# Attention and two mixers on one core: five loads issued ahead of the sixth pair's q and k, and the third pair's score bank opened without twelve products of zeros

## The chip, the core and the metric

The kernel runs on one core of a Trainium2 chip. The metric is the device time of one execution in microseconds; the median of three runs counts. TensorE (PE) multiplies into PSUM banks, VectorE (DVE), ScalarE (ACT) and GpSimd (POOL) work on what it leaves, and SyncE (SP) issues nearly all transfers, in order, to 16 DMA engines.

## The reference

Attention over 4 batches, 8 heads, 576 tokens and 64 numbers a head, once on means of four tokens (repeated to full length) and once on a band of tokens less than 4 apart, the two added; then a mixer over tokens and channels, then a second one with cosines and sines:

```python
out_d = sm_attn(q_d, k_d, v_d)                   # means of 4 tokens
out_up = np.repeat(out_d, factor, axis=2)
mask = np.abs(pos[:, None] - pos[None, :]) < factor
scores = np.where(mask, scale * q @ k.T, -1e9)
out_local = softmax(scores) @ v
x = out_up + out_local                           # (4, 576, 512)
h = relu(xt @ w_tok1) @ w_tok2;  u = x + h.T     # moe
x = u + relu(u @ w_ch1) @ w_ch2
theta = x @ w_theta
y = w_tok_r @ (x * cos(theta)) + w_tok_i @ (x * sin(theta))
out = (x + y) + relu((x + y) @ w_ch)             # moe2
```

The weights come as float64, which the kernel reads as pairs of 32-bit words and turns into float32 itself.

## The kernel before

The attention goes by pairs of heads: 16 pairs, four to a batch. Two pairs make a quad. The work of each pair and quad is cut into steps, written as generators, and the string ORDER (L33) says in which order the steps are taken; the program's instructions stand on each engine in just that order (L1131). A name in ORDER takes the next piece of its step; `L0*2` takes two. The letters that matter here, with the pairs counted from 0, so that pair 5 is the sixth:

- `P5` is load_pair(5) (L375): one transfer of q and k, 128 rows of 1164 float32, into one of four buffers `qk`. The loads stand in the order P0 P1 P4 P2 P3 P5, so P5 is the sixth and takes the buffer of pair 1. It must wait until pair 1's q and k have been read, by pool_pair (DVE) and by the score products (PE).
- `W0` is load_values(0) (L382): four transfers of the values of pair 0, two of 32 rows and two of 6, 1170 float32 each, into one of two buffers `vw`.
- `G0`, `G1` and `G6` are weights of the token mixer (converted, L166): their first piece issues a transfer of float64 (128 rows of 512 words for G0 and G1, of 288 for G6), the later ones turn it into float32 on ACT, DVE and POOL.
- `V1` is pool_values(1) (L391): its first piece loads 128 rows of 1300 float32, the later ones add them up on POOL.
- `K5` is pool_pair(5) (L413): two additions on DVE (L421 and L422) that make sums of four tokens of q and k.
- `F0`, `F1` are quad_front (L425): pooled scores `sd`, their maximum `mxd` (L452), exponentials `pd` (ACT), transpositions `pdt` (L477, L482), the pooled output `od` (L493 to L500), its division `ods` (L504 to L507), and its write and reload (L510 to L519).
- `L1`, `L2`, `L3` are pair_local (L522): local scores `s` of pair 1, 2, 3 in a PSUM room, their maximum and exponentials in `pbuf`, transpositions `pt` (L558), local output `o` (L568).

pair_local opens the room with warm(), which multiplies zeros WARM[n] times into columns that nobody reads, then puts the mask into the room (L530), then adds 40 score products (L533). Each of those is float32 and stands as two products with two weight loads in the trace:

```python
        s = wide(f"s_{at}")
        warm(s[:, 0, 192:512], WARM[n])
        for j in range(2):
            pe.matmul(s[:, j, 0 : NB * W], id16, msk, start=True, stop=False)
        yield
```

The rooms `s`, `sd`, `pdt`, `pt` and `o` come from one pool of two, so each waits until the one before last has been read.

Transfers on SP carry one of eight semaphores, DMAHW0 to DMAHW7, in turn. A transfer waits until the one that had its semaphore before it, eight places ahead, has landed.

Of the kernel before, what the change touches and what calls it, by code (L numbers as in the profile page):

```python
# [30 lines left out]
FIRST = 1  # L31
ROWS = ((8, 9), (0, 2), (4, 6), (2, 3))
ORDER = """  # L33
G3 P0 G2 I*2 P1 G3 P4 G3 V0 P2 G3 K0 G3 G2 I G2 I L0*2 P3 K1 F0 W1 L0 F0 L1 L0 G3 F0 V0 L1*2 P5 V0 L2 W0 G2 K2 V0 G2
F0 G1 L1 V1 F0 L2 K3 G0 G6 K4 L0 F0 L0 L2 L1 G2 F1 L2 K5 L1 L0 F0 F1 G1*2 F1 V1 F0*2 W3 L0 F1 G5 G0 L1 G0 F1 G6 F2 L1
G0 P6 W2 G5 G6 L3 V1 F2 V1 L3 G6 F2 F1 L3 G1 G4 F1 L2 P7 L5 L2 L5 F1 G1 L3 A0 V2 X0 A1 T0 L3 G1 L5 G0 L3 T0 G0 L2 G2
F1 G4 F2 G5 T0 K6 T0 V2 X2 L2 G6 W5 F2 K7 V2 L4*2 E0.0*2 T0 L4 V3 V2 A2 L3 E0.1 L5 G4 L4 W4 L5 G6 L5 G4 L3 X2 F3 G5 P8
P9 A3 G4 F2 G5 E0.1 T1 G4 G5 T0 F2 V3 L4 F3 F2 T0 L4 V3 X2 F3 L6 V3 L6 X7 T0 P11 L6 X2 X0 F3 K8 U0.0 L6 T0 X2 X0 U0.0
# [49 lines left out]
LOWER, WIDE = 2, 2  # L88
MIX = 384
NMIX = 6  # L90
WARM = [24] + [12] * 3 + [0] * 12
DEEP = [4, 4]

B, H, S, D = 4, 8, 576, 64
# [20 lines left out]
def kernel(  # L115
# [177 lines left out]
    def wide(name):  # L293
        return big.tile([128, 2, 512], F32, tag="big", name=name)
# [17 lines left out]
    def warm(out, k):  # L312

        for _ in range(k):
            pe.matmul(out, zero[:, 0:128], zero[:, 0 : out.shape[-1]], start=True, stop=True)
# [206 lines left out]
    def pair_local(n):  # L522
# [4 lines left out]
# [3 lines that stand above are left out]
# [928 lines left out]
```

## Time and profile before

| | us |
|---|---|
| median of three runs | 680.91 (680.24 to 683.12) |
| the profiled execution | 686.51 |
| its span, first to last instruction | 684.7 |
| TensorE busy | 657.2 (96%) |
| VectorE busy | 521.0 (76%) |
| ScalarE busy | 321.1 (47%) |

The profiled execution is one of its own; its time is a little over the median. A row of the timeline gives the start, the time that it took, the engine, the source line, the operation, what it writes and reads, how many instructions were merged, and in brackets the idle time of the engine just before and what ended it. "issue" stands there where the engine waited for nothing that the profile shows. SPq is SP's queue of transfers; its rows give the issue, not the landing. PEclk is the granted clock of TensorE as a share of 2.4 GHz; 0.50 is 1.2 GHz. The attention fills the first part of the span, about 180 us, with the token mixer and the weights mixed in; the rest belongs to the channel mixer and the second mixer.

### The profile page before, as it was taken

How to read it: one execution, taken by the hardware profiler on the slowest of the kernel's cores; microseconds unless marked ns; L12 is line 12 of the kernel's file. 1: busy time of each engine (PE TensorE's matmuls, PEld its weight loads, DVE VectorE, ACT ScalarE, POOL GpSimd, SP SyncE). 2: the span in 40 equal slices, each digit the busy share in tenths (PEclk: the TensorE clock that was granted, in tenths of full speed). 3: DMA queues.
4: the chain of work that ended last, by engine and by line, in shares of the span. 5: the costliest groups of instructions: out<-in, count | busy, mean ns of one | idle time of the engine just before them, and what ended most of it. 6: DMA issues, size and time to landing. Idle time of an engine off the chain costs nothing.

```text
span 684.7 us, 17393 instructions
## 1 busy us (share of the span) xinstructions
PE 657.2 (96%) x7320; PEld 627.6 (92%) x7320; DVE 521.0 (76%) x952; ACT 321.1 (47%) x632; POOL 98.0 (14%) x92
## 2 busy tenths in 40 slices
PE   7678898999999999999999999999999999999997
PEld 4457788989999999999999999999999998998997
DVE  5789997878462679898987886668798848857837
ACT  4466657466252556434624423253657326526311
POOL 3034220604200242300200210012000000000000
PEclk9899999999999999999999999999999999999999
DMA  8688886777441866625353853599620240140202
GB/s 280 198 273 238 255 250 237 209 243 242 137 146 53 285 232 211 226 76 145 128 150 102 279 133 95 178 335 284 169 62 1 75 149 1 61 140 1 70 1 69
DMA packets 93021, 109.93 MB, mean 161 GB/s; under 512 B 46880, under 2 KB 69536, under 8 KB 92944
## 3 DMA queue, kind: packets, MB, share of 16 engines
q1 hardware_dynamic: 92080, 106.08, 49.8%
q0 software_dynamic: 864, 2.75, 1.0%
q8 instruction: 57, 0.93, 0.6%
q14 instruction: 20, 0.16, 0.1%
HBM read 79.13 MB, written 29.69 MB: 159 GB/s over the span
## 4 chain that ended last, share of the span: by engine, by line
PE 83%; DMA 6%; DVE 5%; ACT 3%; SPq 1%; issue 1%; DVEq 0%; ACTq 0%
PE y L158 6%; PE y L157 6%; PE y L159 6%; PE c L158 4%; PE c L157 4%; PE c L159 4%; PE c L699 4%; PE c L702 4%; PE c L700 4%; PE c_p L903 3%; PE c_p L905 3%; PE c_p L902 3%; PE th L158 2%; PE th L157 2%; PE th L159 2%; DMA qk<-qkT 2%
## 5 line engine op out<-in xcount | busy, mean ns | idle before, releaser
L158 PE MATMUL y<-wrl,zh 128*128 128x288 f32 x256 | 74.9, 296 | 0.0
L157 PE MATMUL y<-wrh,zh 128*128 128x288 f32 x256 | 74.8, 296 | 0.0
L159 PE MATMUL y<-wrh,zl 128*128 128x288 f32 x256 | 71.9, 295 | 0.0
L219 POOL TENSOR_TENSOR ww<-ww,raw 128x512 int32<-128x512 int32 (+2 forms) x30 | 41.1, 1373 | 161.8 <-DMA raw<-w_ch 55.6
L157 PEld LDWEIGHTS y<-wrh,zh 128*128 128x128 f32 x256 | 48.0, 188 | 0.0
L158 PEld LDWEIGHTS y<-wrl,zh 128*128 128x128 f32 x256 | 48.0, 188 | 0.0
L159 PEld LDWEIGHTS y<-wrh,zl 128*128 128x128 f32 x256 | 46.9, 188 | 0.0
L219 POOL TENSOR_TENSOR raw<-raw 128x512 int32<-128x512 int32 (+2 forms) x16 | 20.0, 1248 | 139.0 <-DVE raw L215 57.5
L1231 DVE TENSOR_TENSOR cx<-y,cx 128x288 f32<-128x288 f32 x32 | 14.6, 457 | 32.3 <-PE y L159 31.7
L151 ACT CAST cuh<-cx 128x288 fp32r<-128x288 f32 (+1 forms) x16 | 8.8, 553 | 59.5 <-DVE cx L1231 59.5
L199 ACT ACTIVATE ww<-raw 128x512 f32<-128x512 f32 (+2 forms) x30 | 19.4, 647 | 27.1 <-DVE c1l L223 9.5
L921 DVE SCALAR_TENSOR_TENSOR g<-c,g 128x384 fp32r<-128x384 f32 x40 | 21.1, 551 | 13.9 <-ACT g L918 13.8
L157 PE MATMUL th<-thh,cxh 128*128 128x512 f32 (+1 forms) x92 | 31.6, 343 | 0.0
L158 PE MATMUL th<-thl,cxh 128*128 128x512 f32 (+1 forms) x92 | 31.6, 343 | 0.0
L918 ACT ACTIVATE g<-c 128x384 fp32r<-128x384 f32 x40 | 19.1, 490 | 25.5 <-PE c L159 25.5
L159 PE MATMUL th<-thh,cxl 128*128 128x512 f32 (+1 forms) x92 | 31.1, 343 | 0.0
L201 ACT ACTIVATE raw<-raw 128x512 int32<-128x512 uint32 (+3 forms) x46 | 29.4, 639 | 0.0
L929 DVE TENSOR_TENSOR ut<-c,ut 128x384 f32<-128x384 f32 x32 | 17.1, 551 | 9.9 <-PE c L702 9.9
L533 PE MATMUL s<-qk 64*32 64x38 f32 x1280 | 16.1, 205 | 6.1 <-issue 6.1
L533 PEld LDWEIGHTS s<-qk 64*32 64x32 f32 x1280 | 13.6, 105 | 8.8 <-issue 8.4
L157 PE MATMUL t<-w2h,h 128*128 128x256 f32 (+1 forms) x64 | 21.5, 337 | 0.0
L157 PE MATMUL c<-uh,c1h 128*128 128x384 f32 x64 | 21.4, 334 | 0.0
(390 smaller groups left out, 2270.5 us busy)
## 6 DMA issues: line engine op xcount, KB each, us to landing
raw<-w_ch SPq DMA_DIRECT2D x27, 512.0 KB
qk<-qkT SPq DMA_DIRECT2D x16, 582.0 KB
xT<-ut SPq DMA_DIRECT2D x12, 768.0 KB
vd<-vtok SPq DMA_DIRECT2D x8, 650.0 KB
vw<-vloc SPq DMA_DIRECT2D x32, 146.2 KB
uT<-us SPq DMA_DIRECT2D x16, 288.0 KB
ut<-uT SPq DMA_DIRECT2D x6, 768.0 KB
ut<-xT SPq DMA_DIRECT2D x6, 768.0 KB
```

The lines of the kernel that those rows point to most:

```text
L157: pe.matmul(out, lh, rh, start=start, stop=False, skip_group_check=again)
L158: pe.matmul(out, lh, rl, start=False, stop=False, skip_group_check=again)
L159: pe.matmul(out, ll, rh, start=False, stop=stop, skip_group_check=again)
L201: act.activation(f, words[:, :, 0], AF.Copy, scale=2.0**-29)
L219: pool.tensor_tensor(out=w.bitcast(I32), in0=w.bitcast(I32), in1=f, op=ALU.add)
L533: pe.matmul(s[r : r + 32, j, i // 2 * W : i // 2 * W + W], q[64 * j : 64 * j + 64, 32 * g : 32 * g + 32], k[64 * j : 64 * j + 64, 32 * g : ...
L699: pe.matmul(ps[:, 0:MIX], h[:, cb % 2, d], h1, start=cb == cbs[0], stop=False)
L700: pe.matmul(ps[:, 0:MIX], l[:, cb % 2, d], h1, start=False, stop=False)
L702: pe.matmul(ps[:, 0:MIX], weight[cb // 2][2][:, cb % 2, d], h2, start=False, stop=cb == cbs[-1])
L902: pe.matmul(ps[:, 0:MIX], h[:, cb % 2, d], h1, start=cb == cbs[0], stop=False)
L903: pe.matmul(ps[:, 0:MIX], l[:, cb % 2, d], h1, start=False, stop=False)
L921: dve.scalar_tensor_tensor(out=h2, in0=ps, scalar=0.0, in1=h1.bitcast(F32), op0=ALU.max, op1=ALU.subtract)
```

## The change

Two edits. In ORDER, P5 stands later: behind W0, which followed it, and behind the first pieces of G1, G0, G6 and V1, which are pulled forward to stand with it. That makes five steps that issue loads ahead of P5, eight transfers in all. WARM gives pair 2 no products of zeros:

```diff
-G3 P0 G2 I*2 P1 G3 P4 G3 V0 P2 G3 K0 G3 G2 I G2 I L0*2 P3 K1 F0 W1 L0 F0 L1 L0 G3 F0 V0 L1*2 P5 V0 L2 W0 G2 K2 V0 G2
-F0 G1 L1 V1 F0 L2 K3 G0 G6 K4 L0 F0 L0 L2 L1 G2 F1 L2 K5 L1 L0 F0 F1 G1*2 F1 V1 F0*2 W3 L0 F1 G5 G0 L1 G0 F1 G6 F2 L1
+G3 P0 G2 I*2 P1 G3 P4 G3 V0 P2 G3 K0 G3 G2 I G2 I L0*2 P3 K1 F0 W1 L0 F0 L1 L0 G3 F0 V0 L1*2 V0 L2 W0 G1 G0 G6 V1 P5
+G2 K2 V0 G2 F0 L1 F0 L2 K3 K4 L0 F0 L0 L2 L1 G2 F1 L2 K5 L1 L0 F0 F1 G1*2 F1 V1 F0*2 W3 L0 F1 G5 G0 L1 G0 F1 G6 F2 L1
-WARM = [24] + [12] * 3 + [0] * 12
+WARM = [24, 12, 0, 12] + [0] * 12
```

On SP, behind the values of pair 1, before (the names in brackets are the semaphores waited for; qk_1 is the sixth pair's q and k, vw_0 the values of pair 0, raw the weights, vd_1 the pooled values, od_0 the first pooled output):

```order
L378 DMA qk_1_347<-qkT 128x1164 [waits DMAHW6_49,DVE_49,PE_49]
L387 DMA vw_0_366<-vloc 32x1170 [waits DMAHW7_49]
L387 DMA vw_0_366<-vloc 32x1170 [waits DMAHW0_49]
L387 DMA vw_0_366<-vloc 6x1170 [waits DMAHW1_49]
L387 DMA vw_0_366<-vloc 6x1170 [waits DMAHW2_49]
L187 DMA raw_393<-w_tok 128x2x256 [waits DMAHW3_49]
L396 DMA vd_1_396<-vtok 128x1300 [waits DMAHW4_49,Pool_49]
L187 DMA raw_444<-w_tok 128x2x256 [waits DMAHW5_49]
L187 DMA raw_446<-w_tok 128x288 [waits DMAHW6_49]
L510 DMA od_0_57<-ods_0_572 4x32x256 [waits DMAHW7_49,DVE_49]
```

And now, at the same place:

```order
L387 DMA vw_0_352<-vloc 32x1170 [waits DMAHW6_49]
L387 DMA vw_0_352<-vloc 32x1170 [waits DMAHW7_49]
L387 DMA vw_0_352<-vloc 6x1170 [waits DMAHW0_49]
L387 DMA vw_0_352<-vloc 6x1170 [waits DMAHW1_49]
L187 DMA raw_357<-w_tok 128x2x256 [waits DMAHW2_49]
L187 DMA raw_359<-w_tok 128x2x256 [waits DMAHW3_49]
L187 DMA raw_361<-w_tok 128x288 [waits DMAHW4_49]
L396 DMA vd_1_363<-vtok 128x1300 [waits DMAHW5_49,Pool_49]
L378 DMA qk_1_365<-qkT 128x1164 [waits DMAHW6_49,DVE_49,PE_49]
L510 DMA od_0_57<-ods_0_560 4x32x256 [waits DMAHW7_49,DVE_49]
```

The sixth pair's load moved from the first place to the last but one, each of the others one or more places ahead; with its place each transfer changed its semaphore, and so the landing that it waits for.

On TensorE, between the scores of pair 1 and those of pair 2, before:

```order
L533 MATMUL s_1_278<-qk_1_148 32x38 x39
L315 LDWEIGHTS zero [waits DVE_49]
L315 MATMUL s_2_351<-zero 128x320 [waits Activation_49]
...
L530 MATMUL s_2_351<-fixed,id_121 128x190
L477 MATMUL pdt_0_379<-fixed,pd_0_296 128x128 [waits DVE_49,PE_49]
L477 MATMUL pdt_0_379<-fixed,pd_0_296 128x128 x4
L482 MATMUL pdt_0_379<-fixed,pd_0_296 32x128 x8
```

And now:

```order
L533 MATMUL s_1_278<-qk_1_148 32x38 x39
L530 LDWEIGHTS id_121 [waits DVE_49]
L530 MATMUL s_2_349<-fixed,id_121 128x190 [waits Activation_49]
L530 LDWEIGHTS id_121
L530 MATMUL s_2_349<-fixed,id_121 128x190
L477 MATMUL pdt_0_375<-fixed,pd_0_296 128x128 [waits DVE_49,PE_49]
L477 MATMUL pdt_0_375<-fixed,pd_0_296 128x128 x4
L482 MATMUL pdt_0_375<-fixed,pd_0_296 32x128 x8
```

The waits of the first product of zeros went over to the mask's; the transposition's own wait for DVE and PE stayed. On DVE, ACT and POOL the attention's steps stand in the same order as before.

## Rows read from the trace of the kernel before

**Rows 1.** Busy time by stretches: us, each engine's busy (count), PEclk, DMA share, GB/s
```profile
20.00:25.00 5.00, 2.34 (x17) 1.51 (x21) 1.39 (x4) 0.71 (x3) 0.00 (x0) 0.61 1.02 335
25.00:30.00 5.00, 4.81 (x177) 4.06 (x169) 4.11 (x9) 2.38 (x6) 1.60 (x1) 0.71 0.19 64
...
110.00:120.00 10.00, 10.00 (x158) 9.37 (x158) 7.81 (x13) 8.25 (x18) 0.36 (x1) 1.00 0.68 248
```

**Rows 2.** Chain of waits in order of time, 19 to 40 us: start, us, what
```profile
19.04 3.63 issue
...
29.02 0.76 DVE mxd L452
...
35.58 4.70 DMA raw<-w_tok
```

**Rows 3.** Timeline of TensorE's products, 14.9 to 33 us
```profile
14.90 0.31 PE L533 MATMUL s<-qk 64*32 64x38 f32 x17 [0.94 <-issue]
15.14 1.80 PE L315 MATMUL s<-zero 128*128 128x320 bf16 x12
...
16.95 0.71 PE L477 MATMUL pdt<-fixed,pd 128*128 128x128 f32 x5
...
18.16 0.88 PE L533 MATMUL s<-qk 64*32 64x38 f32 x76
22.66 0.34 PE L533 MATMUL s<-qk 64*32 64x38 f32 x4 [3.63 <-issue]
...
32.46 0.76 PE L477 MATMUL pdt<-fixed,pd 128*128 128x128 f32 x5 [2.65 <-ACT pd L473]
```

**Rows 4.** The page: TensorE's counts, instruction queue; that queue from 19.5 to 21.5
```profile
PE 657.2 (96%) x7320; PEld 627.6 (92%) x7320; DVE 521.0 (76%) x952; ACT 321.1 (47%) x632; POOL 98.0 (14%) x92
...
q8 instruction: 57, 0.93, 0.6%
...
q8 instruction: 1, 0.02, 4.1%
```

**Rows 5.** TensorE by microseconds: us, busy (count), PEclk, DMA share, GB/s
```profile
15.00:16.00 1.00, 1.00 (x24) 1.00 0.17 51
...
22.00:23.00 1.00, 0.34 (x5) 0.50 1.06 417
```

**Rows 6.** Timeline of SP, 9 to 45 us: start and time of the issues
```profile
9.87 1.61 SPq L387 DMA_DIRECT2D vw<-vloc  x4
15.31 0.36 SPq L378 DMA_DIRECT2D qk<-qkT  x1
...
18.30 2.26 SPq L187 DMA_DIRECT2D raw<-w_tok  x2
28.27 0.62 SPq L510 DMA_DIRECT2D od<-ods  x1
...
35.58 0.77 SPq L187 DMA_DIRECT2D raw<-w_tok  x1
```

**Rows 7.** Timeline of VectorE, GpSimd and ScalarE, 15 to 41 us
```profile
15.90 0.55 DVE L546 TENSOR_TENSOR pbuf<-s,mx 128x380 f32<-128x380 f32 x1
...
19.73 0.46 DVE L422 TENSOR_TENSOR qkd<-qa 128x288 f32<-128x288 f32 x1
...
25.15 0.75 DVE L421 TENSOR_TENSOR qa<-qk 128x576 f32<-128x576 f32 x1
25.49 1.60 POOL L398 TENSOR_TENSOR vd<-vd 128x650 f32<-128x650 f32 x1 [10.04 <-DMA vd<-vtok]
25.94 1.48 DVE L422 TENSOR_TENSOR qkd<-qa 128x288 f32<-128x288 f32 x1
...
27.75 0.49 DVE L507 TENSOR_TENSOR ods<-od,rd 128x320 f32<-128x320 f32 x1
...
40.30 0.46 ACT L199 ACTIVATE ww<-raw 128x288 f32<-128x288 f32 x1 [4.72 <-DMA raw<-w_tok]
```

**Rows 8.** Waits of SP's queue, 9 to 30 us: us, times, longest
```profile
SPq L187 <- DMA qk<-qkT: 1.5, 1, 1.5
```

## Prediction

> **What bounds the kernel now.** I read the busy time by stretches first. From 110 us on TensorE has no idle time [rows 1], so what happens there is its own work, which the change does not touch. Before that it has, and in the first 45 us a step that comes earlier can bring the rest forward. So I read the chain of waits there [rows 2]. It goes through a stall of 3.63 that the profile calls issue, the maximum of the second pooled scores on VectorE at 29.02, and a load of token weights issued at 35.58 that is waited for 4.70 long. The twelve products of zeros for the third pair lie just ahead of the stall [rows 3].
>
> The stall at 19.04 is not a wait for data: it cuts the 80 products of the third pair's scores into 76 and 4 [rows 3]. From the end of an earlier such gap (14.90) to 19.04 there are 17 + 12 + 2 + 5 + 16 + 76 = 128 products, each with its weight load: 256 instructions. In the whole run the instruction queue q8 moves 57 packets for TensorE's 14640 products and weight loads, 257 each; one of them falls between 19.5 and 21.5 us [rows 4]. So TensorE takes its instructions in blocks of 256, and here it had run out of one. It took 4.1% of 16 engines over 2 us, 1.3 us of one engine, so it was there between 20.8 and 21.5 and TensorE went on 1.2 to 1.9 later.
>
> The DMA engines ran dry just before: at 15 us their share is 0.17 [rows 5], since SP sat from 11.48 to 15.31 at the sixth pair's load [rows 6]. That load needs the buffer of the second pair, whose last reader is the score products that end at 15.21.
>
> **The change part by part.**
>
> *Twelve products of zeros removed.* They take 1.80 on TensorE [rows 3], all of it on the chain. But the next instruction but two is the transposition of the first pooled exponentials, which waits for VectorE too: its bank is the second pair's, whose last reader is the subtraction of 15.90, done at 16.45 [rows 7]. It started at 16.95 [rows 3] and can now start at 16.5. So 0.45 is gained here, not 1.80.
>
> *The block's edge.* 24 instructions fewer put the edge behind the 4 products that were cut off (8 instructions), the five transpositions of the first pair (10) and three products of the pooled output (6). The third pair's scores, whose first 76 ended 2.09 after that transposition began (16.95 to 19.04), are then done near 18.65, not 23.0 (22.66 + 0.34), and VectorE and ScalarE work on them beneath the stall. How long the stall is depends on the packet. It can be asked for at the same moment as before (14.90). In the trace it starts no earlier than 19.5, behind the sixth pair's load, which was issued at 15.31 into empty queues. After the change that load comes last, and the queues are nearly empty about 16 to 17.5, so the packet may go 2 to 3 us earlier. Bounds: TensorE goes on between 19 (packet at once) and 24 (behind two weight blocks more, 1.3 us each at the 417 GB/s of [rows 5]). The pooled output needs 1 to 2 us after that, so it ends between 20 and 26. I take 22.5. Where in this range it is does not matter for what follows, because of the next item.
>
> The Trainium skill's page Runtime: NRT & Kernel Launch (Instruction fetch mechanics) also has 16 KiB blocks of 256 instructions, but says that crossing into the next is mostly hidden. The 3.63 at 19.04 speaks against that here. By the page there would be no stall to shorten, and the sum would be the 0.45 alone.
>
> *Five loads ahead of the sixth pair's.* Every load on SP waits for the one eight places before it; the order shows this as eight names that come round. So the values of the first pair do not all go at 11.5: two pieces do, the third needs the third pair's load, and the fourth the fourth pair's, the last one on SP ahead of the four pieces of 9.87 [rows 6]. The share of 0.17 at 15 to 16 [rows 5], some three engines of 16, says that the data of that time landed between 14.5 and 17. So the fourth piece is issued near 16.5, then the two weight blocks, the short weight block and the pooled values at about 0.45 each, and the sixth pair's load near 18.7, not 15.31. Four loads lie ahead of it: 524 + 524 + 295 + 666 KB, with its own 596 that is 2605 KB (128 rows of 512, 512 and 288 words of 8 bytes, 1300 and 1164 of 4). At 417 GB/s this is 6.3 us. From an issue near 16.9 and the 0.9 us that a load needs to get going (my estimate: the load of 15.31 finds the share still low in the rest of that microsecond), the last byte moves at 24.1. Landing adds 0.7 to 1, and the engine that carries the instruction packets has up to two of them (1.3 each) in its way. So the sixth pair lands between 24.8 and 27.4. Before, it had by 20.2: the short weight block, second of the two issues that begin at 18.30 [rows 6], waits 1.5 for it [rows 8] after the first one's 0.4. I take 26.0, about one packet in the way.
>
> *Who waits for it.* VectorE pools that pair at 25.15, in order ahead of the division of the first pooled output and of the maximum of 29.02. Before, the second half of the pooling took 1.48 where the same form takes 0.46 at 19.73: GpSimd added the pooled values from 25.49 to 27.09 [rows 7]. Those values now land 1.5 us ahead of the sixth pair, so GpSimd is nearly through and I take 0.46. From 26.0: 0.75 + 0.46 = 27.2, then 0.82 for the division (27.42 to 28.24), 28.0 to 28.1. Before: 28.24. **Gain 0.2.** With the bounds: 26.8 to 29.4, a gain of 1.4 or a loss of 1.2.
>
> *What hangs on it.* SP has nothing else from 20.56 until this output: it writes it at 28.27, and what follows, up to the token weights of 35.58 and their first reader at 40.30 [rows 6, 7], is in its queue behind that write. So this chain moves by the 0.2. The maximum of 29.02 follows on VectorE at once: 28.1, a gain of 0.9, and the transposition of 32.46 [rows 3] with it. But ScalarE still meets the token weights at 40.1, so of the 0.9 only the 0.2 is left there.
>
> *The clock.* It was at 1.2 GHz for much of 20 to 30: mean grants of 0.61 and 0.71 there cost 1.95 + 1.45 = 3.4 us of full clock [rows 1]; it fell after TensorE had stood still from 19.04, and was at 0.50 in 22 to 23 [rows 5]. With a shorter stall it may stay up there, but that is worth nothing, since VectorE now waits for the load. After it TensorE runs out of work earlier, at 24 to 27, and waits for the transposition of 32: 5 to 8 us of standing still where it was 2.65. So the fall may come there. What the products between 32 and 40 would lose is between 0 and 3.4. The idle time of 3.63 brought a fall; the one of 2.65 ahead of 32.46 [rows 3] is shorter. I put 0.5 into the sum, as a weight between no fall and a partly hidden one.
>
> **Sum.** -0.2 + 0.5 = +0.3. The profiled execution took 686.51 (span 684.7), 5.6 over the median of 680.91. I put the difference on the median: 681.2.
>
> **The rivals.**
>
> *The load is quick.* It lands at 24.8: no instruction packet in its way, data at the best rate. Then the output is written 1.4 earlier and everything on SP with it, with no fall of the clock: 679.5. For it: DMA engines idle at 15 to 17 that now work. Against: the packet must go by just then. The maximum of 29.02 would come 2.2 earlier; if 1 us more of that is carried than the write gives, 678.5.
>
> *The clock falls at 32.* With the sixth pair at 26 or later TensorE stands still for 5 us and more, and its next products, transposition, local output, pooled scores, run at half speed to about 38. The twelve products of zeros for the fourth pair then warm it again. It decides from where the wait becomes as long as the 3.63 that brought a fall. Price: 3.4 at most; part lies under the token weights of 40.30, so 2.6 beside the gain of 0.2: 683.3, and with the load at 27.4 684.5. The Trainium skill's page TensorE: Matmul & The Clock Gate (Part 1) says the throttled state is the default and activity releases it, a rule against taking zeros away. The rows agree as far as the fall after 19.04 goes.
>
> *The loads do not go ahead.* If the eight names hold the fourth piece to 17.5 and more, the same queue only starts later and the sixth pair lands past 27: the output a full 1.2 late, no gain elsewhere: 682.1.
>
> **How the numbers follow.** Forecast, within about 1 us of 681.2: 0.50. Quick load, 679.5: 0.20. Fall of the clock, 683.3: 0.20. Loads held, 682.1: 0.10. The three runs before lie 2.9 apart (680.24 to 683.12). The range from 678.5 to 684.5 takes in the ends of the outer cases and leaves out what two of them together would do. A change of 0.5%, about what a measurement can tell here, is 3.4: faster than 677.5 needs more than any of my cases gives, 0.06; over 684.3 needs the fall and the late load together, 0.13; within: 0.81.
>
> **What would show it.** In the profile after, the sixth pair's load issued near 18.7, and VectorE's pooling of it waiting for a DMA between 21.8 and 25 to 27, a wait that is not there now. The third pair's maximum near 20, not 23. The cut by issue after the first pair's transpositions, and shorter than 3.63. The first output's write within 1.2 of 28.27. If that write is at 26 or earlier, or 31 or later, the landing was mis-sized. If the time moves by over 3.4 with the write in its place, the cause lies behind 45 us, where I expect nothing, and the prediction is wrong in kind.

## The result, and the profile after

The changed kernel is slower, and outside of the predicted range: a median of 690.21 us (685.73 to 691.74, 7 executions) beside 682.15 for the kernel before, which was 680.91 with the three executions that the forecast started from. The ratio on record is 1.0092 with a 95% interval of 1.0062 to 1.0121; it is estimated from the executions and isn't the quotient of the two medians, which is 1.0118. On another chip (e8_after below) it was 688.63 beside 682.76, 1.0080 (1.0048 to 1.0112). By the ratios the loss is 5.5 to 6.3 us; forecast was 0.3. The ratios leave out executions that lie over 1.5% above the fastest of their kernel, three of the kernel before beside e9_vector_4us and e10_vector_6us and two of e13_before_2us.

The profiled execution took 687.43, one of its shorter ones. SP's timeline in it (start, time, what is issued) shows the fourth piece of the values, the three weight blocks, the pooled values, the sixth pair, and then the first output and the token weights; it answers to [rows 6]:

```profile
17.58 0.27 SPq L387 DMA_DIRECT2D vw<-vloc  x1
17.89 1.50 SPq L187 DMA_DIRECT2D raw<-w_tok  x3
19.49 0.38 SPq L396 DMA_DIRECT2D vd<-vtok  x1
19.98 0.36 SPq L378 DMA_DIRECT2D qk<-qkT  x1
...
30.17 0.62 SPq L510 DMA_DIRECT2D od<-ods  x1
...
37.49 0.35 SPq L187 DMA_DIRECT2D raw<-w_tok  x1
```

The first output is written 1.9 later than in [rows 6], the token weights are issued 1.9 later. The chain of waits of the changed kernel (start, us, what) says why. Where [rows 2] had a stall of TensorE, it now has two landings, the fourth pair's and the sixth's:

```profile
8.79 8.78 DMA qk<-qkT
17.56 0.02 issue
17.58 0.27 SPq L387
...
19.98 8.05 DMA qk<-qkT
28.04 0.02 issue
28.06 0.77 DVE qa L421
28.83 0.02 issue
28.86 0.46 DVE qkd L422
```

The first landing is the one that the fourth piece of the values waits for, by its turn of the eight names. VectorE's timeline has the wait for the second, 5.30, on the pooling, and the division and the second maximum behind it; compare [rows 7]:

```profile
21.19 0.55 DVE L545 TENSOR_REDUCE mx<-s 128x10 f32<-128x380 f32 x1
...
28.06 0.76 DVE L421 TENSOR_TENSOR qa<-qk 128x576 f32<-128x576 f32 x1 [5.30 <-DMA qk<-qkT]
28.86 0.46 DVE L422 TENSOR_TENSOR qkd<-qa 128x288 f32<-128x288 f32 x1
...
29.65 0.49 DVE L507 TENSOR_TENSOR ods<-od,rd 128x320 f32<-128x320 f32 x1
30.05 0.75 DVE L452 TENSOR_REDUCE mxd<-sd 128x4 f32<-128x576 f32 x1
```

TensorE's timeline answers to [rows 3]. The third pair's 80 products are one piece now, a shorter stall stands in the first local output (1.54 here, 2.32 to 3.25 in three more profiles), and behind that TensorE stands for 6.97:

```profile
18.93 0.91 PE L533 MATMUL s<-qk 64*32 64x38 f32 x80
20.13 0.74 PE L558 MATMUL pt<-fixed,pbuf 128*128 128x128 f32 x5 [0.29 <-issue]
...
25.75 0.76 PE L568 MATMUL o<-vw,plt 38*32 38x65 f32 x53 [1.54 <-issue]
33.49 1.33 PE L477 MATMUL pdt<-fixed,pd 128*128 128x128 f32 x5 [6.97 <-ACT pd L473]
```

By stretches of 10 us (us, TensorE's busy time and count, granted clock, DMA share, GB/s), the clock from 30 to 40 is 0.52 after:

```profile
20.00:30.00 10.00, 4.84 (x186) 0.97 0.64 236
30.00:40.00 10.00, 6.51 (x148) 0.52 0.46 144
```

and the same view of the kernel before has its low stretch ahead of that:

```profile
20.00:30.00 10.00, 7.15 (x190) 0.66 0.61 200
30.00:40.00 10.00, 7.30 (x291) 1.00 0.66 210
```

So both rivals that were to cost something, the held loads and the fall of the clock, came about in one execution. The fall isn't all loss, since the kernel before has one of its own, earlier.

### The profile page after: what moved, and what is told of

It reads as the page before. It is cut to its first block, busy times and chain, and to the rows that moved or that the text cites. A ratio compares the mean times of both kernels' runs of the same rounds, so it can differ in the third digit from the quotient of the medians.

```text
span 685.6 us, 17370 instructions
## 1 busy us (share of the span) xinstructions
PE 656.7 (96%) x7308; PEld 626.2 (91%) x7308; DVE 517.9 (76%) x952; ACT 321.2 (47%) x632; POOL 98.6 (14%) x92
## 4 chain that ended last, share of the span: by engine, by line
PE 89%; DMA 4%; DVE 3%; issue 1%; ACT 1%; SPq 1%; POOL 0%; DVEq 0%; POOLq 0%
PE y L158 6%; PE y L157 6%; PE y L159 6%; PE c L157 4%; PE c L159 4%; PE c L158 4%; PE c L699 4%; PE c L702 4%; PE c L700 4%; DMA qk<-qkT 4%; PE c_p L902 3%; PE c_p L905 3%; PE c_p L903 3%; PE t L157 3%; PE th L158 2%; PE th L159 2%
## 5 line engine op out<-in xcount | busy, mean ns | idle before, releaser
L1231 DVE TENSOR_TENSOR cx<-y,cx 128x288 f32<-128x288 f32 x32 | 14.5, 456 | 30.3 <-PE y L159 29.9
L199 ACT ACTIVATE ww<-raw 128x512 f32<-128x512 f32 (+2 forms) x30 | 19.4, 647 | 24.8 <-DVE c1l L223 9.5
L201 ACT ACTIVATE raw<-raw 128x512 int32<-128x512 uint32 (+3 forms) x46 | 29.4, 638 | 0.0
L159 PE MATMUL c<-uh,c1l 128*128 128x384 f32 x64 | 21.4, 334 | 0.0
L158 PE MATMUL c<-ul,c1h 128*128 128x384 f32 x64 | 21.4, 334 | 0.0
```

Of the source, the lines that this page charges most:

```text
L158: pe.matmul(out, lh, rl, start=False, stop=False, skip_group_check=again)
L159: pe.matmul(out, ll, rh, start=False, stop=stop, skip_group_check=again)
L201: act.activation(f, words[:, :, 0], AF.Copy, scale=2.0**-29)
```

## The experiments

Theory 1: the loss comes by the sixth pair, which lands late, through VectorE's queue. Theory 2: it comes by the missing zeros, through TensorE's clock or its blocks of instructions. The table has the kernels that were timed in turns with the kernel before, each beside it on the same chip; the clock is the mean of the granted clocks of the executions in the ratio, and the first write is that of the profiles. The kernel before had a clock of 0.987 to 0.988 in these comparisons, and its medians on the different chips were 681.3 to 685.2, so only ratios are compared.

| kernel | loads, zeros, what else | first write | ratio (95%) | clock |
|---|---|---|---|---|
| e3_before | as before | 27.8 | 1.0009 (0.9983 to 1.0035) | 0.9875 |
| e8_after | the change | 29.8 | 1.0080 (1.0048 to 1.0112) | 0.9825 |
| e1_loads | loads of after, zeros of before | 29.8 | 1.0057 (1.0026 to 1.0088) | 0.9833 |
| e2_zeros | loads of before, zeros of after | 24.3 | 0.9995 (0.9971 to 1.0020) | 0.9866 |
| e4_k5 | after, sixth pooling later | 22.5 | 1.0002 (0.9979 to 1.0026) | 0.9840 |
| e7_k5_zeros | e1_loads, sixth pooling later | 22.9 | 0.9995 (0.9967 to 1.0023) | 0.9875 |
| e6_behind_values | after, sixth load earlier | 23.7 | 0.9999 (0.9970 to 1.0027) | 0.9871 |
| e9_vector_4us | e6, five additions more | 28.3 | 1.0047 (1.0014 to 1.0081) | 0.9829 |
| e10_vector_6us | e6, eight additions more | 30.9 | 1.0093 (1.0061 to 1.0125) | 0.9818 |
| e5_busy | after, 48 products of zeros more | 30.8 | 1.0170 (1.0128 to 1.0212) | 0.9817 |
| e13_before_2us | before, three additions more | 26.4 | 1.0078 (1.0042 to 1.0113) | 0.9852 |

### Which half of the change makes the loss

e1_loads is the changed kernel with `WARM = [24] + [12] * 3 + [0] * 12`, so only the loads move. e2_zeros is the kernel before with `WARM = [24, 12, 0, 12] + [0] * 12`. e8_after is the changed kernel itself.

> The five loads ahead of the sixth pair's, and the twelve products of zeros kept. If the move of the loads makes the loss (theory 1), the time is that of the changed kernel, 688 to 692, with the sixth pair issued near 20, landed near 28 and the first output written near 30. If the zeros make it (theory 2: without them TensorE's clock falls), 681 to 684. If each makes a part, between: 685 to 688.

> The loads in the old order, and the third pair's room opened without the twelve products of zeros. Theory 1 (the loads): 681 to 683.5, 0.45 of gain at the first pooled transposition at most. Theory 2 (the zeros): 687 to 691, with a low granted clock between 10 and 40 us. Parts: 683.5 to 687.

> The changed kernel once more, beside the others on one chip. The same loss as in the first comparison: ratio 1.006 to 1.010, a mean clock near 0.981, the first output written near 30. If the zeros taken away add to the loss of the loads, it stays above the 1.0057 of e1_loads; if they don't, it comes near it.

The loads alone cost 0.57% (687.16, in the range where each half was to make a part), the zeros alone nothing that can be measured (683.89, which is among the times expected if each made a part, but the kernel before took 684.15 beside it). Together they cost 0.80%, and the intervals of e1_loads and e8_after overlap, so that the zeros add something to the loads isn't shown. In e1_loads, VectorE's timeline has the same wait, with the zeros kept:

```profile
27.68 0.76 DVE L421 TENSOR_TENSOR qa<-qk 128x576 f32<-128x576 f32 x1 [6.29 <-DMA qk<-qkT]
```

e2_zeros has no stall of 3.63: its timeline shows one of 0.67 within the pooled output, which then ends by 23.3, and one of 2.15 at the next edge, in the first local output:

```profile
21.97 0.42 PE L493 MATMUL od<-vl,pts 128*32 128x260 f32 x3 [0.67 <-issue]
...
27.52 1.09 PE L568 MATMUL o<-vw,plt 38*32 38x65 f32 x53 [2.15 <-issue]
```

Its first output is written at 24.29, 4.0 earlier than in [rows 6], and it is no faster for it. Its granted clock was low from 10 to 40 (0.86, 0.84 and 0.79 by stretches of 10), as theory 2 has it, but without a loss. Theory 2 falls as the main cause.

### Taking the late load off VectorE's path

e4_k5 and e7_k5_zeros leave the load where the change puts it and move its reader on VectorE behind the division, the second maximum and the first local output (e7 keeps the zeros, so that TensorE has the instructions of the kernel before):

```diff
-F1 L2 K5 L1 L0 F0 F1 G1*2 F1 V1 F0*2 W3
+F1 L2 L1 L0 F0 F1 G1*2 F1 V1 F0*2 K5 W3
```

e6_behind_values leaves VectorE alone and issues the load behind the values, with three weight blocks and the pooled values no longer ahead of it:

```diff
-V0 L2 W0 G1 G0 G6 V1 P5
+V0 L2 W0 P5 G1 G0 G6 V1
```

> The changed kernel with the sixth pair's pooling on VectorE moved behind the division of the first pooled output, the second maximum and the first local output's division. Nothing on VectorE stands behind the late load then. If the loss goes by VectorE's queue (theory 1), the first output is written near 24 to 26 and the time falls to 680 to 684. If it goes by TensorE's clock or its instruction blocks (theory 2), the write comes early as well, but the time stays at 687 to 691.

> The five loads ahead, the twelve products of zeros kept, and the sixth pair's pooling moved behind the second maximum as in e4_k5. TensorE's blocks of instructions then end where they end in the kernel before. If only VectorE's queue matters: ratio 0.999 to 1.001, as e4_k5. If the shifted block edges of e4_k5 ate a gain of its early output (write at 22.5, 5.8 earlier than before, and no gain in time): faster than before, 0.994 to 0.998.

> The changed kernel with the sixth pair's load right behind the values, ahead of three weight loads and the pooled values: one load ahead of it, not five. Its issue still waits for the fourth piece of the values, near 17.6. If the landing decides (theory 1): it lands 2 to 4 us earlier, 24 to 26, the first output is written at 26 to 28, and the time is that of the kernel before within 0.2%. If it is enough that the load leaves its old place (it then starts 2.6 us later than before in any case): ratio 1.004 and more.

All three bring the loss back to nothing: 684.65, 683.40 and 681.97, ratios of 1.0002, 0.9995 and 0.9999. In e4_k5, VectorE's timeline shows the division at 21.59, and the sixth pair landing as late as in the changed kernel, with little behind it:

```profile
21.59 0.16 DVE L504 TENSOR_SCALAR rd<-od 128x5 f32<-128x5 f32 x1
...
28.04 0.76 DVE L421 TENSOR_TENSOR qa<-qk 128x576 f32<-128x576 f32 x1 [2.01 <-DMA qk<-qkT]
```

In e6_behind_values the pooling doesn't wait at all. SP's and VectorE's timelines: issued at 17.47, read at 21.57, so it was there within 4.1, where behind four more transfers it needed 8.05. That is earlier than the 24 to 26 expected, and so is the write.

```profile
17.47 0.36 SPq L378 DMA_DIRECT2D qk<-qkT  x1
...
23.68 0.61 SPq L510 DMA_DIRECT2D od<-ods  x1
```

```profile
21.57 0.76 DVE L421 TENSOR_TENSOR qa<-qk 128x576 f32<-128x576 f32 x1
```

So theory 1 holds: what costs isn't the load's new place as such, but that VectorE stands waiting for its landing with the first output behind it. The hope that an early output makes a version faster than the kernel before fell with the same three kernels: they write 4.6 to 5.8 earlier than [rows 6] and take the same time.

### The same delay without a late load

e9_vector_4us and e10_vector_6us are e6_behind_values with the first addition of the sixth pair's pooling done six and nine times over, so that VectorE is late by work of its own. Nothing changes on the queues, nor in TensorE's instructions:

```diff
-        dve.tensor_tensor(out=h, in0=src[:, :, :, 0:2], in1=src[:, :, :, 2:4], op=ALU.add)
+        for _ in range(6 if n == 5 else 1):
+            dve.tensor_tensor(out=h, in0=src[:, :, :, 0:2], in1=src[:, :, :, 2:4], op=ALU.add)
```

> e6_behind_values with five more first additions of the sixth pair's pooling on VectorE (each 0.76, written over with the same sums), so that the division of the first pooled output and the second maximum come 3.8 later, with nothing changed on the queues and on TensorE. The write goes from 23.7 to 27.5, near the 28.3 of the kernel before. Theory 3a (delay of VectorE at 22 to 30 is carried to the end one for one, and the kernel before is usually earlier than in its two profiles): 685.5 to 687. Theory 3b (up to about 28 there is slack, something later ends last): 682 to 683.

> As e9_vector_4us with eight more additions, 6.1 later: the write at 29.8, as in the changed kernel. Both theories: the time of the changed kernel if the delay on VectorE is all of it, 687.5 to 690. If the late load costs by something else (transfers that collide behind it), clearly less: below 686.

VectorE's timeline in e10_vector_6us, with the nine additions:

```profile
21.41 7.13 DVE L422 TENSOR_TENSOR qa<-qk 128x576 f32<-128x576 f32 x9
28.58 1.48 DVE L423 TENSOR_TENSOR qkd<-qa 128x288 f32<-128x288 f32 x1
```

A write at 30.9 gives 1.0093, the changed kernel's loss, with the sixth pair landed early. From 23.7 to 28.3 the ratio rises by 0.0048, to 30.9 by 0.0094: 3.3 us for 4.6 and 6.4 for 7.2, so some 0.7 to 0.9 of each microsecond arrives at the end. The intervals of the ratios leave room for 0.1 to 1.4 by the first pair and 0.5 to 1.3 by the second. Theory 3a, one for one, fits that; what it says of the kernel before is looked at next.

### How late is "late"? More profiles of both kernels

By that rate the change, whose first write is 1.9 later, should cost under 2. So the two kernels were profiled again, e3_before, e11_before, e12_before and e17_before as they were, e14_after and e15_after, and e16_loads for e1_loads.

> The kernel before, profiled once more. Its profiled execution took 686.51 where its other runs took 680.2 to 684.2. If the stall of 3.63 at 19.04 and the clock of 0.66 between 20 and 30 us belong to that one execution, another profile has a shorter stall, a clock above 0.9 there and a span near 680; if they belong to the kernel, the same rows come back. Time 681 to 684 in either case.

> A third profile of the kernel before. Theory 3a: in an execution of 682 to 684 the stall at 19 is shorter than 3.63 and the first output is written before 27. Theory 3b: the stall and the write at 28 come back whatever the time.

> A fourth profile of the kernel before, for the same question: how far the stall at 19, the write and the granted clock of 20 to 55 us go together with the time.

> A fifth profile of the kernel before. If the stall at 19 is a matter of the execution: none or a short one in an execution under 681, 3 or more in one above 682. If it always comes back: 3 or more, the write at 27 to 28.

> Another profile of the changed kernel. If its first output is usually written later than in the two profiles seen (30.17, 29.75): near 32 in an execution of 690 and more. If not: near 30 again, and the rest of the loss lies behind it.

> A fourth profile of the changed kernel, for the same question: the write near 30 whatever the time, or later where the time is longer.

> A second profile of the kernel with the five loads ahead and the zeros kept. The first took 683.73, the lowest of its 12 executions, with the write at 29.78. If the write is what sets the time, it is later here in a longer execution; if the granted clock behind 27 us does, the write is near 29.8 again and the clock is lower.

The stall belongs to the kernel before, whatever the time. In these four executions of 686.14, 682.09, 684.45 and 682.74 it was 3.63, 3.08, 3.36 and 3.35, the write at 27.75, 26.93, 27.72 and 28.14. By the letter e11_before fits theory 3a (a stall under 3.63, a write ahead of 27), by little. The guess that the usual execution has no stall was wrong. TensorE's timeline in the shortest of them, e11_before:

```profile
17.87 0.87 PE L533 MATMUL s<-qk 64*32 64x38 f32 x76
21.82 0.26 PE L533 MATMUL s<-qk 64*32 64x38 f32 x4 [3.08 <-issue]
```

The view of the tile `ods` has the first and the last of the eight output writes in one line (ns: least, median, most; start of the first and of the last). From the last one the end is 505 to 506 away in every profile of these two kernels, so all that differs lies ahead of it. Kernel before, as first profiled:

```profile
L510 SPq DMA_DIRECT2D od<-ods x8: 580/584/616, 28.3 to 179.3; - x8
```

Changed kernel, as first profiled:

```profile
L510 SPq DMA_DIRECT2D od<-ods x8: 579/584/616, 30.2 to 180.7; - x8
```

Over the five profiles of the kernel before, the first write is at 27.8 on average and the last at 177.1 (174.8 to 179.3); over the four of the changed kernel at 30.3 and 180.7 (178.0 to 182.2). So the first comes 2.5 later and the last 3.5. The second is 2.3 later (43.9 for 41.6), the third 3.4 (66.4 for 63.0): what comes on top of the late first write comes between the second write and the third. The times of e14_after and e15_after, 684.92 and 689.13, don't follow their first writes, 30.95 and 30.34; e16_loads writes 1.07 later than e1_loads, at a mean clock of 0.983 for 0.990, and took 2.8 longer. Profiles of a few executions that scatter over 4 us can't say more than that: the write is near 30 as a rule, not near 32, and what is lost beyond it lies behind it.

### Does the clock make the rest?

e5_busy adds 48 products of zeros behind the first local output, into columns that nobody reads.

```diff
+        if n == 0:
+            rest = blocks(room, STEP)[:, 0:NB, 65:STEP]
+            for _ in range(48):
+                pe.matmul(
+                    rest,
+                    zero[:, 0:128],
+                    zero[:, 0 : NB * (STEP - 65)].rearrange("p (b n) -> p b n", b=NB),
+                    start=True,
+                    stop=True,
+                )
```

> The changed kernel with 48 more products of zeros behind the first local output, into columns that nobody reads, so that TensorE works for some 4.6 us of the 7 that it waits for the second pooled transposition. Theory 1a (the late load costs by the clock that falls in this wait): the granted clock stays at 1.00 from 30 to 40, the mean clock comes back to 0.985 or more, and the time falls by 2.5 to 4, to a ratio near 1.003. Theory 1b (it costs by its delay alone, which the chain carries to 110 us): the clock may rise, but the ratio stays at 1.006 to 1.010.

It missed both expectations: 694.53, 1.0170. TensorE's timeline shows the zeros, and a stall of 2.78 where the changed kernel has one of 0.95:

```profile
26.58 5.80 PE L579 MATMUL o<-zero 128*128 128x185 bf16 x48
34.14 0.76 PE L477 MATMUL pdt<-fixed,pd 128*128 128x128 f32 x5 [1.75 <-ACT pd L473]
...
45.20 0.32 PE L498 MATMUL od<-vl,pts 128*32 128x65 f32 x1 [2.78 <-issue]
```

In the stretches of 10 us the clock is indeed back from 30 to 40:

```profile
30.00:40.00 10.00, 7.63 (x176) 0.95 0.41 127
40.00:50.00 10.00, 6.60 (x230) 0.73 0.76 229
```

but it is low later, and the mean clock of the timed executions, 0.9817, is no better. What it does show is small: the fourth pair's score products began 9.56 behind the first write with the clock up (40.37), and 10.29 to 10.84 behind it in the four profiles of the changed kernel, so the low clock of 30 to 40 costs some 0.7 to 1.3 up to there. What it costs behind is not told apart from the block edges that 96 more instructions move: this test of the clock decides nothing.

What stays is a correlation. Most kernels that lose have the lower mean clock (table), but e4_k5 has 0.9840 (0.9868 for the kernel before beside it) and loses nothing. For e8_after, 0.9877 less 0.9825, times 685, is 3.6 us of full clock, of some 5.5 lost. Within the twelve executions of e1_loads, the time falls by 6.8 us for each 0.01 of clock; 0.01 of 685 us is 6.85. That is the closest case, not the rule: the slope is 5.0 in e8_after, 2.5 in the 35 executions of the kernel before beside e1_loads, and there is none in e3_before. The falls aren't the change's alone either. From 30 to 40 the clock is 0.52 to 0.65 in the four profiles of the changed kernel, but 0.66 in two of the five of the kernel before (e12_before, e17_before), and 0.70 and 0.68 in e4_k5 and e7_k5_zeros, which lose nothing. That the longer wait of TensorE is what lowers it in the changed kernel is likely, but no run here shows it by itself.

### A delay in the kernel before

e13_before_2us does the first addition of the sixth pair's pooling four times in the kernel before, with loads and zeros as they were; e18_before_2us is a second profile of it.

> The kernel before with three more first additions of the sixth pair's pooling on VectorE, 2.3 later: the first output is written near 30, as in the changed kernel, with the loads in the old order and the zeros kept. If a delay at this place is carried one for one: 2 to 2.5 more than before, ratio 1.003 to 1.004. If the lateness by itself makes the whole loss: 1.007 to 1.010. If the new order of loads is needed for a loss: below 1.002.

> A second profile of the kernel before with three more additions on VectorE. With the stall at 19 back: the write near 30 and 686 or more. Without it: the write near 26.5 again and 678 to 682.

It didn't make the lateness that it was to make. TensorE's timeline in e13_before_2us has the third pair's products uncut, with the loads in the old order:

```profile
18.79 0.91 PE L534 MATMUL s<-qk 64*32 64x38 f32 x80
19.99 0.74 PE L559 MATMUL pt<-fixed,pbuf 128*128 128x128 f32 x5 [0.29 <-issue]
...
25.81 0.86 PE L569 MATMUL o<-vw,plt 38*32 38x65 f32 x65 [1.84 <-issue]
```

The write came at 26.45, and at 25.85 in e18_before_2us, earlier than in all five profiles of the kernel before; yet the median is 685.59 beside 681.31, and the ratio 1.0078. The stall isn't gone but comes one block later, in the first local output: 1.84 here and 2.55 in e18_before_2us, where the kernel before has 0.24 at most. The instruction packet that TensorE waits for at 19 began to move (queue q8, by half microseconds) between 19.0 and 20.0 in the five profiles of the kernel before and in e2_zeros, and between 16.0 and 16.5 in these two. Why it moves earlier here, with the load in its old place and three more instructions on VectorE only behind that time, isn't explained.

Where the time goes can be read off these two profiles of one kernel. They took 678.54 and 685.68; the second was expected at 678 to 682. Up to the second output's write they are level (39.91 and 39.32); the third is at 59.42 and 63.88. In between (us, TensorE's busy time and count, granted clock, DMA share, GB/s), e13_before_2us:

```profile
40.00:60.00 20.00, 16.09 (x502) 1.00 0.88 267
```

and e18_before_2us, where TensorE stood by issue for 2.72 ahead of 43.46 and ran at 1.2 GHz from 44 to 54 (0.50 to 0.53):

```profile
40.00:60.00 20.00, 14.55 (x387) 0.74 0.69 227
```

So some 5 of the 7.1 between them arise there, behind the first two writes, by a stall at a block's edge and a low clock together. Which of the two weighs more isn't told apart.

That a kernel with an early write loses 0.78% also limits the reading of e9_vector_4us and e10_vector_6us, which add such instructions as well: that a delay is carried is shown by e1_loads against e7_k5_zeros and by e8_after against e4_k5, which only move the pooling; the rate of 0.7 to 0.9 is not as firm.

## Why the prediction was wrong, point by point

**The twelve zeros, right.** The first pooled transposition now waits 1.05 for VectorE's subtraction, as said, and e2_zeros gives nothing that can be measured beside the 0.45 of gain that were put down.

**The block's edge, half right.** The edge moved to where it was put: in e2_zeros the cut stands two products into the pooled output, three were forecast, and TensorE went on at 21.97, within 19 to 24. In the changed kernel the block was there in time and only the next edge shows, 1.54 at the first local output. Its reason, a packet behind the sixth pair's load that can go 2 to 3 earlier without it, is borne out in part: the packet began to move at 19.0 to 20.0 in the five profiles of the kernel before and in e2_zeros, at 16.0 to 18.5 in all twelve with the load moved. But e13_before_2us and e18_before_2us have it at 16.0 with the load in its old place. And what was saved at this edge came back at the next: 1.54 to 3.25 in the changed kernel's four profiles.

**The issue of the sixth pair, the first step that failed.** The eight names worked as described, but the fourth piece of the values went at 17.58, not at 16.5, since the fourth pair needed until 17.56 to land, and the three weight blocks took 1.50 with the pooled values behind them. So the load went at 19.98 (20.2 to 20.6 in the other three profiles), not at 18.7, with the weight blocks ahead of it 1.0 late. The share of 0.17 in one microsecond was a poor base for the landing of one transfer: it says how much moves, not whose last byte.

**The landing, the term that was mis-sized.** From the issue, 7.3 were taken and 8.05 needed. It landed at 28.0 (27.6 to 28.9 in the other three), outside of the bounds of 24.8 and 27.4. With the top of its own terms, 1 for landing and two packets, the upper bound would have been 27.7 and not 27.4. The "loads held" rival had this case, at a tenth of the chance, and put the write 1.2 late; it was 1.9.

**VectorE, right but for that.** The second addition took 0.46, and the division followed at once. The write at 30.17 is outside of 26.8 to 29.4 by what the landing was. By the prediction's own signs it lies in between, neither within 1.2 of 28.27 nor at 31 or later.

**What hangs on it, the step that let the sum go wrong.** The chain on SP moved one for one, as said: token weights 1.9 later. The price of the clock was given as well, 2.6 to 3.4, and the fall came. But they stood as separate cases, with 0.10 and 0.20, and the range was told to leave out "what two of them together would do". The four cases take up the whole chance, and yet 0.13 is given to times over 684.3, which "needs the fall and the late load together": the joint case was seen, and had no place in the sum. Yet the late landing is what makes TensorE stand for 7 us, so they belong together. With the prediction's own prices, 1.8 for the landing (2.0 later than taken, less the gain of 0.2) and 2.6 to 3.4 for the clock, the sum would have been 4.4 to 5.2, near the 5.5 and more that were measured. That this sum comes near isn't proof of its second half: e5_busy had the clock up from 31 to 43 and was no faster, and what the change adds to the falls that the kernel before has isn't measured by itself. Part of the loss also arises between the second write and the third (44 to 66), where the prediction expected nothing.

**The clock's condition, wrong.** The fall was to hang on a wait as long as the 3.63 that brought one, with 2.65 too short. In e12_before and e17_before the same wait was 2.55 and 2.63, and the transposition behind it took 1.33 for 0.76, at 1.2 GHz. So a fall at 32 is no new cost of the change in each execution.

**The measure.** The profiled execution of 686.51 was put 5.6 over the median as if it were odd. Four more profiles of the same kernel look the same, at 682.1 to 686.1; single executions of it scatter from 677 to 690. The stall and the late write were its rule.

**What stays open.** Shown is that the loss goes by the late load and what stands behind it on VectorE; how 2.5 at the first write become 5.5 at the end is not. Kernels that write their first output at 22 to 24 (e2_zeros, e4_k5, e6_behind_values, e7_k5_zeros) are no faster than the kernel before, which writes at 27.8. Their profiles show where the lead goes: by the second write, at 38.2 to 40.3 for 41.6 on average, 1.4 to 3.4 of the 3.5 to 5.2 are left, by the third between nothing and 3.4. The cuts by issue, which sit elsewhere in each kernel, with the low clock behind them, are a candidate, as e13_before_2us and e18_before_2us show between two executions of one kernel; and e13_before_2us says that they don't follow from the order of the loads alone.

## What to carry to other kernels

When a load is moved behind others, look first for who reads it in order on an engine, and what stands behind that reader: moving the reader, or the load four transfers further ahead, was worth the whole 0.8% here. Take a queue's waits by turn (here every eighth transfer) from the landing of the very transfer that holds the turn, bounded by its slowest reading, and add up the rivals that one event may bring about together rather than giving each a chance of its own. A stall that a profile shows is not a gain to be had: e2_zeros cut 3.63 down to 0.67, had 2.15 at the next edge, and gave nothing.

## What was not expected of the hardware

TensorE's stalls at the edges of its blocks, 3.08 to 3.63 in five profiles of five of the kernel before, depend on things far from them: with twelve products fewer, another order of loads, or three instructions more on VectorE the one at 19 is 0.9 or less, and one of 1.5 to 3.3 stands at the next edge, in the first local output, in all fifteen other profiles. And a load of the same size needed 4.1 at most from issue to its reader with one transfer of values just ahead of it, 8.05 with three weight blocks and the pooled values in between. The Trainium skill's page Runtime: NRT & Kernel Launch (Instruction fetch mechanics) holds that a crossing into the next block is mostly hidden; these rows show that here the first 50 us don't bear that out.
